# Batch 0's middle feature by the FFT, folds kept out of steps with DFT sums, loads behind the gate, gathers on SyncE's queue

## The chip, the cores and the metric

The kernel runs on one core of a Trainium2 chip. A core has five engines with instruction queues of their own: TensorE (PE: matmuls, with weight loads shown apart as PEld), VectorE (DVE), ScalarE (ACT), GpSimd (POOL) and SyncE (SP, which here only issues DMA transfers). ScalarE and GpSimd issue transfers as well. An engine works through its queue in order, so an instruction that waits holds all that stand behind it. The metric is the device time of one execution in microseconds, lower is better.

## The reference, cut to what matters

```python
x: (8, 3136, 256) float32            # B, S, D
X = np.fft.fft(np.fft.fft(x, axis=1), axis=2).real       # over the sequence, then over the features
h = np.maximum(X @ w_in, 0.0)                             # w_in: (256, 1024)
conv = conv_w[0] * h[s-1] + conv_w[1] * h[s] + conv_w[2] * h[s+1]   # per channel, zero beyond the ends
out = (h * (1 / (1 + np.exp(-conv)))) @ w_out             # w_out: (1024, 256)
```

The three weights arrive as float64, and the kernel narrows them itself.

## The kernel before, in words

**The transform.** The real part of the two-dimensional transform is a cosine-cosine sum minus a sine-sine sum. The kernel uses the symmetries of both. For one batch, rows n of x are folded with their mirror rows (S/2-n and so on) and feature d with feature D-d; what is left are 8 groups of 98 or 99 rows by 128 features, in two tiles `w` per batch. These `fold_ops` (line 143) are 14 pieces per batch, seven for each half h of the rows, nearly all of it VectorE (lines 158 to 187). Then 8 units of four matmuls each (`units`, line 272) multiply the folded rows with cosine and sine tables `tab` over the sequence ("DFT sums"; they accumulate in the single PSUM bank `pd`, for batch 0 in banks `po`); each unit ends with a copy on ScalarE (`u.copy`, lines 287, 306) and two VectorE instructions (`u.fin`, lines 291 to 324) that write a quarter of the rows `pt` (cosine part) and `qt` (sine part), 128 features by 1569 frequencies. The transform over the features is merged into w_in: `G` is the feature table `dm` times w_in (`blocks`, line 589).

**Feature D/2 = 128** has no partner in the fold. Its cosine transform over the sequence is one row of 1569 numbers per batch, and its share of the result is that row times one column `ge` per channel (`column`, line 606). There are two ways to the row in the kernel before:
- Batches 1 to 7: `Feature` (line 374). The 3136 values of one batch are gathered from HBM as a 56 by 56 matrix (`gather`, line 417: 3136 pieces of 4 bytes, issued from ScalarE's queue). Four stages follow: matmul, multiply by twiddles on VectorE, four matmuls, copy and store on ScalarE (lines 443 to 463). `place` (line 380) and `tables` (line 423) prepare its small tables in steps 5 and 11 to 13. Batches 1 to 3 are gathered in step 7, 4 to 7 in step 20.
- Batch 0: the fold keeps x[:, 128] apart (`ea`), `feature` (line 327) multiplies it by the cosine table in 8 small matmuls, GpSimd joins the parts in `er`, `flip` and `store` finish the row.

From the DRAM row `ed`, `spread` (line 465) broadcasts a chunk to all 128 partitions, `eb`. In every step ScalarE then writes eb times ge into the PSUM bank `pa` (`seed`, line 635), and the matmuls add to it. The first four steps of batch 0 have no seed: a fourth matmul with `er` and `left` stands in (lines 661, 662), since the row is not there yet.

**The steps.** The rest is a loop over 256 steps, written out by hand (lines 861 to 885): 8 batches, 4 chunks of the mirrored frequencies (CUTS, line 34), 8 channel tiles. A batch is 32 steps (`per`). For step t the engines get, in this order of the program:
- ScalarE: sigmoid of step t-2 (line 713), copies of the products of step t+1 (line 677, for the first 20 steps lines 672 and 674), the seed of step t+2 (line 643), the first tap of the convolution of step t (line 694).
- VectorE: two additions that make h for k and S-k (line 688), work on the side ("dve"), two further taps of step t-1 (line 700), half of the gating product of step t-2 (line 721).
- GpSimd: the other half of the gating product (line 720).
- TensorE: the products of step t+1 into `pb` and `pa`, six (in the last chunk of odd batches seven) matmuls with w_out of step t-3 into `po`, and at the end the side work "pe": DFT sums of the next batch.

The side work is placed by the dictionary `side`: `at(step, where, fn)`. Where "load" stands, transfers are issued: plain loads and broadcasts from SyncE's queue, and four indirect loads of mirrored rows per half batch from GpSimd (line 133). In the kernel before, "load" stands ahead of "dve" and so ahead of the gate on GpSimd's queue. Folds of batch b run from the end of those of b-1 up to step `stop` (20, 44, 68, 98, 130, 162, 194), its DFT sums from there to step 32b-3 (lines 810 to 841), so that folds of one batch and sums of another share steps.

**The head.** Ahead of the loop: x of batch 0 and the tables are loaded, and a memset on GpSimd (line 577) holds the tables behind the loads of x on SyncE's queue; 16 matmuls keep TensorE busy (`keep_on`, line 750); the folds, the DFT sums of batch 0 and the narrowing of the weights (`narrow`, lines 517 to 524, seven VectorE instructions for 512 columns) follow.

Of the kernel before, what the change touches and what calls it, by code (L numbers as in the profile page):

```python
# [9 lines left out]
F32 = mybir.dt.float32  # L10
# [20 lines left out]
FIRST = 4  # L31
# [7 lines left out]
def kernel(  # L39
# [33 lines left out]
    ep = ctx.enter_context(tc.tile_pool(name="ep", bufs=2))  # L73
    erp = ctx.enter_context(tc.tile_pool(name="erp", bufs=1))
# [28 lines left out]
    xh, wt, ea = {}, {}, {}  # L103
# [3 lines left out]
    sg = const.tile([P, 2, 2], F32, name="sg")  # L107
    nc.gpsimd.memset(sg[:, 0], -1.0)
    nc.gpsimd.memset(sg[:, 1], 1.0)
# [33 lines left out]
    def fold_ops(b):  # L143
# [3 lines left out]

        def half(h):
# [27 lines left out]
            def feats(odd):  # L176
                def f():
                    if h == 0 and odd:
                        wt[b] = [wp.tile([P, 4, HQ, P], F32, name="w", tag="w%d" % i) for i in range(2)]
                        if b == 0:  # L180
                            ea[b] = ep.tile([P, 2, HQ], F32, name="ea", tag="ea")
                            nc.gpsimd.memset(wt[b][0][0:KR, 2:4, :, P - 1:P], 0.0)
# [6 lines left out]
                    if b:  # L189
                        nc.gpsimd.memset(wt[b][odd][k, 2:4, qs, P - 1:P], 0.0)  # L190
                    elif odd:
                        gt(w[k, 2:4, qs, P - 1], t()[k, 7:5:-1, :, P], sg[k], op=ALU.mult)
                    else:
                        nc.gpsimd.tensor_copy(ea[b][k, :, qs], v[:, :, :, P])
# [10 lines left out]
    PQ, eb, er = {}, {}, {}  # L205
# [36 lines left out]
    class Unit:  # L242

        def __init__(self, b, mms, copy, fin, own=False):
            self.own, self.b, self.mms, self.copy_, self.fin_ = own, b, mms, copy, fin

        def matmuls(self, i, n):
            if i == 0:
                self.p = spare() if self.b == 0 and not self.own else psd.tile([P, 512], F32, name="pd", tag="pd")
# [22 lines left out]
    def units(b):  # L272
# [54 lines left out]
        def feature():  # L327

            mms = []
            for i in range(2):  # L330
                for j, qs in enumerate(((3, 1), (2, 0))):
                    for c in range(2):
                        n = HO // 2 + 1 - c
                        o = 32 * (2 * j + c)
                        mms.append(product((slice(o, o + 1), slice(0, n)),
                                           lambda k, q, c=c: ea[b][0:k, c, q:q + 1], 0, qs[i],
                                           slice(c, HE, 2), i == 0, i == 1))

# [613 lines left out]
```

## Time and profile before

| what | value | where from |
|---|---|---|
| median of 3 runs | 1238.14 us (1236.81 to 1238.31) | the times |
| the profiled execution | 1238.29 us, of it span 1236.5 us | the times and the page |
| TensorE busy | 1189.9 us, 96% | page, part 1 |
| VectorE busy | 1136.0 us, 92% | page, part 1 |
| ScalarE busy | 878.1 us, 71% | page, part 1 |
| GpSimd busy | 378.4 us, 31% | page, part 1 |
| chain that ended last | TensorE 71%, VectorE 18%, issue 4%, ScalarE 3% | page, part 4 |
| granted TensorE clock | 0.996 over the span | the times |

All times inside the profile count from the start of the span; 1.8 us of the execution lie outside it. "Busy" for TensorE is not TensorE at its peak, because matmuls overlap and their ends are modelled. The 32nd, 64th, ... gating product of VectorE (line 721) ends at 236.9, 384.8, 530.4, 674.9, 819.5, 964.0 and 1104.1 us; these marks cut the trace into stretches of 32 steps. The first gating product ends at 65.6 us.

### The profile page before, as it was taken

How to read it: one execution, taken by the hardware profiler on the slowest of the kernel's cores; microseconds unless marked ns; L12 is line 12 of the kernel's file. 1: busy time of each engine (PE TensorE's matmuls, PEld its weight loads, DVE VectorE, ACT ScalarE, POOL GpSimd, SP SyncE). 2: the span in 40 equal slices, each digit the busy share in tenths (PEclk: the TensorE clock that was granted, in tenths of full speed). 3: DMA queues.
4: the chain of work that ended last, by engine and by line, in shares of the span. 5: the costliest groups of instructions: out<-in, count | busy, mean ns of one | idle time of the engine just before them, and what ended most of it. 6: DMA issues, size and time to landing. Idle time of an engine off the chain costs nothing.

```text
span 1236.5 us, 15434 instructions
## 1 busy us (share of the span) xinstructions
PE 1189.9 (96%) x4876; PEld 908.4 (73%) x4876; DVE 1136.0 (92%) x1696; ACT 878.1 (71%) x1832; POOL 378.4 (31%) x474
## 2 busy tenths in 40 slices
PE   5998989899999999999999999999999999999998
PEld 4666667677777777677777777777777777777776
DVE  7799979999999989999999999999899888899996
ACT  2467646686677776777777777787777777788884
POOL 5225431433324241342324223242122211222222
PEclk9999999999999999999999999999999999999999
DMA  9504241211222120210212111120001000110000
GB/s 226 183 7 79 79 55 46 85 28 52 65 66 76 33 65 14 75 56 26 79 38 67 31 52 52 45 86 26 9 18 52 31 26 27 39 39 27 26 27 30
DMA packets 70213, 66.30 MB, mean 54 GB/s; under 512 B 28123, under 2 KB 57827, under 8 KB 70131
## 3 DMA queue, kind: packets, MB, share of 16 engines
q1 hardware_dynamic: 42443, 52.09, 13.7%
q0 software_dynamic: 5120, 12.85, 3.5%
q10 hardware_dynamic: 22568, 0.36, 1.3%
q8 instruction: 39, 0.64, 0.2%
q14 instruction: 43, 0.35, 0.1%
HBM read 39.53 MB, written 25.74 MB: 53 GB/s over the span
## 4 chain that ended last, share of the span: by engine, by line
PE 71%; DVE 18%; issue 4%; ACT 3%; DMA 1%; ACTq 0%; SPq 0%; DVEq 0%
PE po L94 43%; PE pb L94 10%; PE pa L94 10%; PE pd L94 7%; DVE g L700 6%; DVE g L721 2%; DVE h L688 2%; DVE xh L158 2%; ACT nb L677 1%; DVE w L187 1%; DVE xh L169 1%; DVE w L186 1%; DMA xh<-in_x_dram 1%; ACT g L713 1%; ACTq L419 0%
## 5 line engine op out<-in xcount | busy, mean ns | idle before, releaser
L94 PE MATMUL po<-wout,g 128*128 128x256 f32 x3072 | 711.6, 381 | 18.2 <-DVE g L721 18.2
L94 PEld LDWEIGHTS po<-wout,g 128*128 128x128 f32 x3072 | 580.8, 190 | 173.0 <-DVE g L721 50.0
L700 DVE SCALAR_TENSOR_TENSOR g<-h,cw,g 128x770 f32<-128x770 f32 (+1 forms) x512 | 555.5, 1085 | 9.8 <-ACT g L694 0.7
L720 POOL TENSOR_TENSOR g<-g,h 128x385 f32<-128x385 f32 (+1 forms) x256 | 241.0, 942 | 793.3 <-ACT g L713 536.3
L713 ACT ACTIVATE g<-g 128x385 f32<-128x385 f32 (+2 forms) x512 | 244.4, 527 | 200.7 <-DVE g L700 199.5
L677 ACT ACTIVATE nb<-pb 128x386 f32<-128x386 f32 (+2 forms) x472 | 208.2, 494 | 81.4 <-PE pb L94 80.5
L688 DVE CUSTOM_DVE_ANT_0 h<-pa,nb 128x386 f32<-128x386 f32 (+2 forms) x492 | 255.5, 559 | 3.7 <-ACT h L674 3.7
L694 ACT ACTIVATE g<-h,cw 128x770 f32<-128x770 f32 (+1 forms) x256 | 243.6, 951 | 0.2 <-DVE h L688 0.2
L94 PE MATMUL pa<-pt,G 128*128 128x387 f32 (+2 forms) x512 | 212.5, 496 | 7.5 <-ACT pa L643 7.5
L94 PE MATMUL pb<-qt,G 127*128 127x387 f32 (+2 forms) x512 | 212.6, 496 | 0.0
L643 ACT ACTIVATE pa<-eb,ge 128x387 f32<-128x387 f32 (+2 forms) x252 | 151.8, 603 | 15.8 <-issue 11.6
L94 PEld LDWEIGHTS pa<-pt,G 128*128 128x128 f32 x512 | 96.6, 189 | 82.1 <-issue 18.6
L721 DVE TENSOR_TENSOR g<-g,h 128x385 f32<-128x385 f32 (+1 forms) x256 | 145.4, 568 | 1.4 <-ACT g L713 1.4
L94 PE MATMUL pd<-tab,w 98*128 98x196 f32 (+3 forms) x448 | 120.9, 374 | 0.0
L94 PEld LDWEIGHTS pb<-qt,G 127*128 127x128 f32 x512 | 94.7, 190 | 17.4 <-issue 1.0
L133 POOL DMA_INDIRECT xh<-in_x_dram,idx x64 | 97.9, 1529 | 15.4 <-issue 13.0
L94 PEld LDWEIGHTS pd<-tab,w 98*128 98x128 f32 (+1 forms) x448 | 83.6, 190 | 12.7
L740 ACT COPY os<-po 128x256 f32<-128x256 f32 x196 | 58.2, 394 | 8.5 <-PE po L94 5.5
L158 DVE TENSOR_TENSOR xh<-xh 98x1020 f32<-98x1020 f32 (+1 forms) x32 | 46.7, 1465 | 3.8 <-DMA xh<-in_x_dram,idx 3.8
L169 DVE TENSOR_TENSOR xh<-xh 98x1024 f32<-98x1024 f32 (+1 forms) x32 | 40.6, 1269 | 0.1
L188 POOL COPY w<-xh 98x4 f32<-98x4 f32 (+1 forms) x32 | 27.4, 856 | 13.3 <-DVE xh L174 7.4
L291 DVE TENSOR_TENSOR qt<-as,pd 128x197 f32<-128x197 f32 (+1 forms) x14 | 7.2, 514 | 19.9 <-ACT as L287 19.9
(114 smaller groups left out, 392.8 us busy)
## 6 DMA issues: line engine op xcount, KB each, us to landing
out_dram<-os SPq DMA_DIRECT2D x192, 128.0 KB
xh<-in_x_dram SPq DMA_DIRECT2D x16, 784.0 KB
eb<-ed SPq DMA_DIRECT2D x16, 193.5 KB
tab<-dft_seq_dram SPq DMA_DIRECT2D x4, 589.5 KB
raw<-in_moe_w_in_dram SPq DMA_DIRECT2D x4, 512.0 KB
raw<-in_moe_w_out_dram SPq DMA_DIRECT2D x1, 2048.0 KB
eb<-ed SPq DMA_DIRECT2D x8, 209.0 KB
eb<-ed SPq DMA_DIRECT2D x8, 193.0 KB
```

Of the source, the lines that this page charges most:

```text
L94: nc.tensor.matmul(o, l, r, start=start, stop=stop, skip_group_check=True)
L133: nc.gpsimd.indirect_dma_start(out=xh[b, h][0:NP, 7 - m].rearrange("p q d -> p (q d)"), out_offset=None, in_=bass.AP(tensor=x.tensor, offs ...
L158: vt(a[:, :, :, 1:D], a[:, :, :, 1:D], r[:, :, :, D - 1:0:-1], op=ALU.add)
L643: act(pa[s][:, 0:n], eb[b, c], AF.Copy, scale=ge[:, f:f + 1])
L677: act(nb[s][:, i, cols], p[:, cols], AF.Copy, scale=-1.0 if i else 1.0)
L688: nc.vector._custom_dve(TENSOR_ADD_SAT, out=to, in0=a[:, cols], in1=c[:, i, cols], s0=BIG, s1=0.0)
L694: act(gs[s], hs[s][:, 0:n], AF.Copy, scale=cw[:, 0, s[2]:s[2] + 1])
L700: stt(out=g, in0=h[:, k:k + n], scalar=cw[:, k, f:f + 1], in1=g, op0=ALU.mult, op1=ALU.add)
L713: act(gs[s][:, c], gs[s][:, c], AF.Sigmoid)
L720: gt(g[:, p], g[:, p], h[:, p], op=ALU.mult)
L721: vt(g[:, v], g[:, v], h[:, v], op=ALU.mult)
L740: nc.scalar.copy(out=osb[:, j % 2], in_=pt[:, j % 2])
```

## The change

- Batch 0's row for feature D/2 comes from `Feature` too. `place` and `tables` move into the head, as does one gather; stages 0 and 1 are put between the folds (after 11 of 14 pieces), stage 2 behind `keep_on`, stage 3 behind the first `mirror_tables`. `feature`, `row`, `flip`, `store`, `ea`, `er` and the fourth matmul of the first four steps go, and these steps get seeds like all others. `keep_on` is 8 matmuls of 512 columns in place of 16 of 256, two of them into the two `pa` banks; the matmuls that had started those banks (`start_all`) go.
- On SyncE's queue the broadcast of batch 0's first chunk is put ahead of the loads of `dm` and of w_in's parts 1 to 3, which had stood directly behind the tables. The columns of `ge` for the first channel tiles are computed ahead of the loop.
- All gathers are issued from SyncE's queue, one per step (steps 6 to 8 and 21 to 24).
- "load" is run behind the gate instead of ahead of "dve", and the loads of a half batch are spread over one step each.
- The ends of the folds are 20, 46, 72, 98, 125, 157, 189. A fold piece of batch 2 or later takes the next step that holds no `u.fin`, no stage 1 of `Feature` and no other fold piece (`free`). The steps of the folds become: batch 2: 20, 28, 30, 31, 33 to 40, 42, 44; batch 3: 46, 48, 50, 52, 54, 56, 58, 60, 62, 63, 64, 66, 68, 70; batch 4: 72, 73, 75, 78, 80, 81, 83, 86, 88, 89, 91, 92, 94, 96; and so on. Batch 1's stay in steps 9 to 19.

```diff
-FIRST = 4
-                        if b == 0:
-                            ea[b] = ep.tile([P, 2, HQ], F32, name="ea", tag="ea")
-                            nc.gpsimd.memset(wt[b][0][0:KR, 2:4, :, P - 1:P], 0.0)
...
-                    if b:
-                        nc.gpsimd.memset(wt[b][odd][k, 2:4, qs, P - 1:P], 0.0)
-                    elif odd:
-                        gt(w[k, 2:4, qs, P - 1], t()[k, 7:5:-1, :, P], sg[k], op=ALU.mult)
-                    else:
-                        nc.gpsimd.tensor_copy(ea[b][k, :, qs], v[:, :, :, P])
+                    nc.gpsimd.memset(w[k, 2:4, qs, P - 1:P], 0.0)
...
-        def gather(self, b0, b1):
-            for b in range(b0, b1):
-                nc.scalar.dma_start(out=self.y[self.K, b - b0].unsqueeze(2), in_=bass.AP(
-                    tensor=x.tensor, offset=x.offset + b * S * D + P,
-                    ap=[[RC * D, RC], [D, RC], [1, 1]]))
+        def gather(self, b, b0):
+            nc.sync.dma_start(out=self.y[self.K, b - b0].unsqueeze(2), in_=bass.AP(
+                tensor=x.tensor, offset=x.offset + b * S * D + P, ap=[[RC * D, RC], [D, RC], [1, 1]]))
...
+    feat = Feature()
     w_cv.load(nc.scalar)
+    feat.place()
     for h in range(2):
         for f in load_ops(0, h, nc.sync, nc.scalar, h == 1):
             f()
+    feat.gather(0, 0)
 
     nc.gpsimd.memset(tabs[1][0:1, 0, 0, 0:1], 0.0)
     load_tables(1)
     w_in[0].load(nc.sync)
     load_tables(0)
-    nc.sync.dma_start(out=dm, in_=dft_dim[:, :, 0:2])
-    for i in (1, 2, 3):
-        w_in[i].load(nc.sync)
...
-        if not first(s):
-            if s in ((0, 0, FIRST), (0, 0, FIRST + 1)):
-                start_all(pa[s].rearrange("p (t n) -> p t n", t=2), dm[:, 0, 0], w4[0])
-            act(pa[s][:, 0:n], eb[b, c], AF.Copy, scale=ge[:, f:f + 1])
+        act(pa[s][:, 0:n], eb[b, c], AF.Copy, scale=ge[:, f:f + 1])
...
-        if first(s):
-            mm(pa[s][:, 0:n], left[0:1, f, :], er[b][:, ch.k0:ch.k1], False, False)
...
-    for f in fold_ops(0):
+    for i in range(3):
+        feat.tables(i)
+    begin, us = units(0)
+    begin()
+    ops = fold_ops(0)
+    for f in ops[0:11]:
         f()
+    feat.stage(0, 0, 1)
+    feat.stage(1, 0, 1)
+    for f in ops[11:]:
+        f()
 
-    odds = [us[j] for j in (0, 1, 5, 6)]
+    odds = [us[j] for j in (0, 1, 4, 5)]
     w_in[0].narrow(0, 2)
-    keep_on(16)
+    keep_on([idle] * 6)
+
+    keep_on([psa.tile([P, 512], F32, name="pa", tag="pa") for _ in range(2)])
+    feat.stage(2, 0, 1)
     mirror_tables(0)
+    feat.stage(3, 0, 1)
+    spread(0, [0])
+    nc.sync.dma_start(out=dm, in_=dft_dim[:, :, 0:2])
+    for i in (1, 2, 3):
+        w_in[i].load(nc.sync)
...
-    flip()
-    store()
-    spread(0, range(len(chunks)))
+    spread(0, range(1, len(chunks)))
     for f in load_ops(1, 0, nc.sync):
         f()
+    column(0)
     blocks(0)
...
+    ends = [9] + [max(26 * b - 6, per * (b - 1) - 3) for b in range(1, B)]
+    taken = set()
+
+    def free(cycle):
+
+        while cycle in taken:
+            cycle += 1
+        taken.add(cycle)
+        return cycle
+
+    for c, b0, b1 in ((6, 1, min(4, B)), (21, 4, B)):
+        for b in range(b0, b1):
+            at(c + b - b0, "load", lambda b=b, b0=b0: feat.gather(b, b0))
+    for c, b0, b1 in ((14, 1, min(4, B)), (per - 1, 4, B)):
+        for i, where in enumerate(("pe", "dve", "pe", "act")):
+            at(c + i + (i > 2), where, lambda i=i, b0=b0, b1=b1: feat.stage(i, b0, b1))
+        taken.add(c + 1)
...
+        c0, n = ends[b - 1], ends[b] - ends[b - 1]
+        cs = [free(c0 + j * n // len(ops)) if b > 1 else c0 + j * n // len(ops) for j in range(len(ops))]
...
+                for j, fn in enumerate(load_ops(b + 1, h, nc.sync)):
+                    at(cs[7 * h + 6] + 1 + j, "load", fn)
...
         if t < n:
             combine(steps[t])
-        run("load")
         run("dve")
...
         if 0 <= t - 2 < n:
             gate(steps[t - 2])
+        run("load")
         if t >= LAG:
             mm2(steps[t - LAG])
         run("pe")
```

## The prediction

> **What bounds the kernel now.** I read the page first, for the two engines that are nearly full, then the busy time in stretches of 32 steps (their marks are in the section above), then the places where TensorE stands idle, in order of time. From the page:
>
> ```profile
> PE 1189.9 (96%) x4876; PEld 908.4 (73%) x4876; DVE 1136.0 (92%) x1696; ACT 878.1 (71%) x1832; POOL 378.4 (31%) x474
> ...
> PE 71%; DVE 18%; issue 4%; ACT 3%; DMA 1%; ACTq 0%; SPq 0%; DVEq 0%
> ```
>
> TensorE bounds most of the span, but not all: 18% of the chain is VectorE. Where, the stretches tell (start:end, length, busy time of PE, PEld, DVE, ACT, POOL, then granted clock, DMA share, GB/s):
>
> ```profile
> 65.60:236.90 171.30, 157.87 (x633) 115.75 (x631) 158.06 (x224) 108.02 (x236) 62.48 (x73) 0.99 0.28 59
> 236.90:384.80 147.90, 145.99 (x595) 112.06 (x596) 140.70 (x214) 108.12 (x224) 47.61 (x60) 0.99 0.16 50
> 384.80:530.40 145.60, 141.90 (x580) 108.15 (x579) 137.60 (x210) 107.40 (x224) 49.55 (x59) 1.00 0.19 58
> ...
> 819.50:964.00 144.50, 142.60 (x588) 109.98 (x588) 135.20 (x208) 107.73 (x224) 37.96 (x50) 1.00 0.10 32
> 964.00:1104.10 140.10, 140.10 (x582) 109.11 (x581) 120.36 (x185) 107.44 (x224) 29.08 (x40) 1.00 0.10 30
> ```
>
> The stretch from 964.00 has DFT sums but no folds, and TensorE never stops: 140.1 us is what TensorE needs for an even batch. An odd one has 8 more output matmuls of 0.43 us, 3.5 us, so 143.6. Against these floors the stretches from 236.9 on (147.9, 145.6, then 144.5, 144.6, 144.5) stand 4.3, 5.5, 0.9, 4.5 and 0.9 us too high: 16.1 us is all that better placed folds can bring there. The first stretch has VectorE and TensorE equally full and 13.4 us of idle TensorE. Its largest piece, from the timeline (start, us, engine, line):
>
> ```profile
> 157.16 2.90 ACTq L419 DMA_DIRECT2D ft<-in_x_dram  x1
> ...
> 160.10 4.58 ACTq L419 DMA_DIRECT2D ft<-in_x_dram  x2
> ...
> 164.74 0.59 ACT L643 ACTIVATE pa<-eb,ge 128x387 f32<-128x387 f32 x1 [6.78 <-issue]
> ...
> 165.38 1.36 PE L94 MATMUL pa<-pt,G 128*128 128x387 f32 x2 [3.78 <-ACT pa L643]
> ...
> 166.53 4.04 PE L94 MATMUL po<-wout,g 128*128 128x256 f32 x12
> ```
>
> ScalarE issues four gathers, stands 6.78 us behind them, and the seed (L643) comes late; TensorE waits 3.78 us for it. Then its clock is down: the stretch 165 to 170 shows a granted 0.66, and twelve records that take 2.75 us elsewhere take 4.04, the two before them 1.36 instead of 0.81. The stall costs 3.78 + 1.29 + 0.55 = 5.6 us.
>
> What a fold does in a step with sums, VectorE's timeline in step 54:
>
> ```profile
> 326.93 1.02 DVE L688 CUSTOM_DVE_ANT_0 h<-pa,nb 128x386 f32<-128x386 f32 x2
> 328.97 0.36 DVE L310 TENSOR_TENSOR as<-as,pd 128x196 f32<-128x196 f32 x1 [1.02 <-ACT as L306]
> 329.25 0.35 DVE L312 TENSOR_TENSOR as<-as,pd 128x196 f32<-128x196 f32 x1
> 329.52 0.68 DVE L186 TENSOR_TENSOR w<-xh 98x508 f32<-98x508 f32 x1
> 330.12 0.68 DVE L187 TENSOR_TENSOR w<-xh 98x508 f32<-98x508 f32 x1
> 330.71 2.07 DVE L700 SCALAR_TENSOR_TENSOR g<-h,cw,g 128x770 f32<-128x770 f32 x2
> 332.70 0.56 DVE L721 TENSOR_TENSOR g<-g,h 128x385 f32<-128x385 f32 x1
> ```
>
> The end of the sums waits for ScalarE's copy (1.02 us), which waits for TensorE; so VectorE is tied to TensorE there, and the fold of 1.3 us lies on the way to the taps and the gate. The step takes 6.24 us from gate to gate, its neighbours without side work 3.43. The next steps with a fold alone take about 4.7, which TensorE's step (six output matmuls 2.59, two products 1.30, some 0.5 of sums) nearly covers.
>
> **The head, part by part.** Its chain: the tables land, ScalarE mirrors (L239), TensorE sums, VectorE narrows and finishes.
>
> ```profile
> 26.05 8.10 PE L94 MATMUL po<-tab,w 98*128 98x196 f32 x32
> ...
> 36.65 0.88 PE L94 MATMUL pd<-tab,ea 99*1 99x197 f32 x16
> ...
> 46.04 0.91 PE L94 MATMUL pa<-er,left 1*128 1x386 f32 x2
> ...
> 58.17 0.56 DVE L688 CUSTOM_DVE_ANT_0 h<-pa,nb 128x385 f32<-128x385 f32 x1 [2.82 <-ACT h L674]
> ```
>
> *Added.* `place` on GpSimd took 1.93 us in step 5 (76.61 to 78.54) and now stands ahead of the eight indirect loads of x; the memset that releases the tables follows these, so the tables are issued at 14.8 instead of 12.90. One gather goes ahead of them: four gathers filled the DMA engines from 155 to 170 us (shares 0.97, 0.95 and 0.46 of 5 us, 11.9 us), less about 3.4 us for the 0.8 MB of x in the first of these stretches: 2.1 us each. The small tables (0.18 MB at the head's 240 GB/s) are 0.8 us. The engines were idle for parts of the first 12 us, so these overlap: the tables come between 1.5 and 4 us later, I take 2.7. TensorE's sums then start at 28.7 instead of 26.05. Stages 0 to 3 themselves are short (matmuls of 0.3 us, products 0.5 x 2 on VectorE, ACT copy 0.3) and lie in waits for the tables; four more seeds on ScalarE (0.59 each) lie in its idle time, as it is busy 6.5 of the 15 us from 40 to 55. If that cover is gone they cost 2.4.
>
> *Moved on SyncE's queue.* The broadcast of chunk 0 waits for the store of stage 3: `mirror_tables` ends at 25.9 + 2.7 = 28.6, copy and issue 0.6, and 1.6 to land (the row's store of before was issued at 43.39, the broadcast behind it at 44.96): 31. Behind it stand `dm`, three parts of w_in and w_out. Part 1 (0.26 + 0.52 MB at 240 GB/s, 3.3 us, and 1.6 to land) is there at 36; VectorE narrows it at 36.28 + 2.7 = 39. It is covered by 3 us.
>
> *Removed.* On TensorE 0.88 (`ea`), four products of 0.65, two blocks of about 0.43 and two starts of 1.02, some 6 us, most of it between 44 and 64 us, where VectorE waits: 2.82 us at 58.17 and 0.84 at 48.42. VectorE's chain from 26 to 58 us is otherwise full, so it moves by +2.7 and loses 3.66 in waits; I keep 0.25 of that as lost to the new order and book **-0.7 us** (between +1 and -3).
>
> **The loop.** *Gathers.* The second group saves **-5.6 us** (-3.5 if the sums behind it, where TensorE is the bound, take part of it back; -7.3 if VectorE's own idle time counts). The first group (5.29 us of ScalarE at 89.72) meets a stretch where VectorE is full with narrowing; VectorE waited 0.50 there (at 96.53), and 0.17 of `place` (L402) leaves its way: **-0.7** (0 to -3, as TensorE lost 2.83). The seven transfers now hold SyncE, whose next work, stores and broadcasts, is steps away. Here the Trainium skill speaks against the edit: "DMA: Bandwidth & Descriptors", section "Issuing engines are not separate DMA queues", says that all queues share the same 16 engines and that another issuer saves only the sequencer's issue time, usually small. By the rule these two items are worth about 0 and the sum below would be 1229. The row decides: the issue held ScalarE for 5.29 and 8.3 us, presumably at the pace at which the pieces were moved, and SyncE can stand that.
>
> *Loads behind the gate.* GpSimd's loads (median 1.50 us) no longer delay its gate product (0.87). No instruction of TensorE waits longest for L720 before, so nothing is gained: 0. What is late now is the load itself, by one step of 4.5; the fold that uses the tile is seven pieces away.
>
> *Folds.* Collisions of fold and sums: about five per batch go, at about 0.9 us each (the excess of 4.5 in an even stretch over five). But folds are packed: VectorE per stretch is 24 x 3.43 + 8 x 3.72 = 112.1 plus 1.31 per piece (9.15 us for seven) plus 7.4 for sums. Stretch by stretch:
> - 236.9: 20 pieces, VectorE 146.5 with the two stage-1 products: it, not TensorE, is the bound. It was 147.9 with 19 pieces, of which a step with a fold and stage 1 at 231 to 237 cost a clock drop (0.74). I take 146.4: **-1.5** (+3 to -4.3).
> - 384.8: 17 pieces, VectorE 141.8 and waits: 143.6, **-2.0** (0 to -5.5).
> - 530.4: floor 143.6 plus a little, **-0.7**; 819.5 the same, **-0.7**.
> - 674.9: 14 pieces, VectorE 137.8, so TensorE's 140.1 plus 0.9: **-3.6** (-1 to -4.5).
> - From 964 no folds, before and after: 0. In steps 20 to 29 TensorE is the bound with its dense sums, so four pieces fewer there bring nothing.
>
> **Sum.** -0.7 - 5.6 - 0.7 - 1.5 - 2.0 - 0.7 - 3.6 - 0.7 = -15.5 us. The profiled execution took 1238.29, 1236.5 in the span; that it stands 0.15 above the median of the runs is nothing. 1238.3 - 15.5 = **1222.8 us**.
>
> **Rivals.**
> 1. *VectorE becomes the bound.* Ten folds in the eleven steps from 30 to 40 need 4.74 us a step where TensorE needs 3.9, 8 us in all; waits at the end of the sums add 1 us each time. Then the stretches from 236.9 give nothing together, and the gathers and the head remain: -7.0, **1231**. For it: DVE 140.70 of 147.90. Against it: VectorE may lag by more than a step before TensorE starves.
> 2. *Everything reaches its floor.* All of the 16.1, the whole 7.3 and 1 to 3 more in the head: **1213**. Against it: 17 and 20 pieces in a stretch.
> 3. *SyncE's queue stalls the head, slower.* Place: the broadcast that waits for the stored row, with part 1 of w_in behind it. Price: one us of the head for each us after the 3 us of cover. With 15.5 us of gain elsewhere it decides when the row lands later than about 49 us instead of 31; 23 us of delay give **1243**. Nothing in the trace has a small store land so late.
> 4. *No change.* The stall is given back: TensorE is full with sums in steps 20 to 29 whoever issues, and the head loses 4 us: **1238**. Against it: the 3.78 us of idle TensorE and the clock.
>
> **How the numbers follow.** This kernel's measurement can tell about 0.2%, 2.5 us. Chances: forecast 0.62 (own range 1217 to 1229), rival 1 0.2, rival 2 0.1, rival 3 0.04, rival 4 0.04. The range 1213 to 1233 leaves out some of rivals 2, 3 and 4 and the far end of 1. Faster 0.93, within 0.03, slower 0.04.
>
> **What would show it.** After: no idle of ScalarE for issue longer than 1 us; no step with a PE clock of 0.66; the five middle stretches at 146, 144, 144, 141 and 144; TensorE's sums in the head at 28 to 29; VectorE's wait of 2.82 gone. It is wrong if sums start later than 31, if w_in's part 1 holds VectorE, or if TensorE's waits for L721 grow in steps 30 to 45.

## The result and the profile after

| | before | after |
|---|---|---|
| median of the runs | 1238.22 us (1236.81 to 1238.47) | 1227.74 us (1226.35 to 1228.34) |
| ratio to before, 95% interval | | 0.9916 [0.9899, 0.9933] |
| the profiled execution, and its span | 1238.29, 1236.5 us | 1227.89, 1226.1 us |

The kernel is 10.5 us faster; 15.5 had been forecast. From the page of the kernel after, busy times and shares of the chain that ended last:

```profile
PE 1180.9 (96%) x4834; PEld 900.0 (73%) x4834; DVE 1126.7 (92%) x1698; ACT 876.0 (71%) x1830; POOL 362.1 (30%) x466
...
PE 71%; DVE 21%; issue 4%; ACT 2%; DMA 1%; POOL 0%; DVEq 0%; SPq 0%; POOLq 0%; ACTq 0%
```

TensorE still does most of the chain; VectorE's share has gone up from 18% to 21%, although it has less to do. Where the time went is read from the stretches of 32 steps, cut at the same gating products as before (columns: start:end, length, busy time of PE, PEld, DVE, ACT, POOL, granted clock, DMA share, GB/s):

```profile
69.30:231.10 161.80, 152.77 (x620) 112.20 (x620) 150.21 (x216) 103.09 (x213) 52.41 (x60) 1.00 0.21 51
231.10:379.80 148.70, 145.25 (x592) 110.38 (x592) 141.25 (x217) 107.58 (x225) 54.30 (x64) 1.00 0.19 60
379.80:525.30 145.50, 142.48 (x581) 108.25 (x580) 138.47 (x212) 107.40 (x225) 44.09 (x58) 1.00 0.18 57
525.30:670.50 145.20, 144.94 (x599) 111.66 (x599) 137.56 (x212) 107.42 (x225) 53.21 (x60) 1.00 0.17 56
670.50:813.20 142.70, 141.49 (x582) 108.63 (x581) 134.65 (x207) 108.08 (x224) 45.78 (x56) 1.00 0.16 52
813.20:956.00 142.80, 142.52 (x590) 110.51 (x589) 131.42 (x205) 108.00 (x224) 30.31 (x48) 1.00 0.08 29
956.00:1093.80 137.80, 137.80 (x570) 107.10 (x569) 121.03 (x183) 106.73 (x224) 30.78 (x40) 1.00 0.09 30
```

Set against the stretches before, and against the forecast:

| part | before | forecast | after | after less before |
|---|---|---|---|---|
| up to the first gating product | 65.6 | 64.9 | 69.3 | +3.7 |
| first stretch | 171.3 | 165.0 | 161.8 | -9.5 |
| second | 147.9 | 146.4 | 148.7 | +0.8 |
| third | 145.6 | 143.6 | 145.5 | -0.1 |
| fourth | 144.5 | 143.8 | 145.2 | +0.7 |
| fifth | 144.6 | 141.0 | 142.7 | -1.9 |
| sixth | 144.5 | 143.8 | 142.8 | -1.7 |
| seventh | 140.1 | 140.1 | 137.8 | -2.3 |
| last | 132.4 | 132.4 | 132.3 | -0.1 |

The parts add up to the spans, 1236.5 and 1226.1 us, and differ by 10.4. So three things need an answer: a head that lost 3.7 us instead of winning 0.7, a first stretch that won 3.2 more than booked, and stretches two to seven, where the folds act, that won 4.5 us instead of 8.5.

The gathers did what was said. SyncE's timeline of the kernel after, where the last three gathers of the second group are issued (start, us, engine, line):

```profile
162.92 5.27 SPq L361 DMA_DIRECT2D ft<-in_x_dram  x3
```

TensorE's timeline of the kernel after, same place:

```profile
162.64 0.82 PE L91 MATMUL pa<-pt,G 128*128 128x387 f32 x2
163.29 2.75 PE L91 MATMUL po<-wout,g 128*128 128x256 f32 x12
165.88 2.80 PE L91 MATMUL pd<-tab,w 98*128 98x392 f32 x8
```

They hold SyncE for 5.27 us, and nothing on TensorE waits: there is no bracket with an idle time in these rows, and twelve output matmuls take 2.75 us again instead of 4.04.

The head did not. The chain that ended last, followed through the head of the kernel after (start, us, what):

```profile
8.87 12.15 DMA ft<-in_x_dram
21.15 0.59 PE pd L91 x2
21.74 8.53 PE pb L91 x12
30.28 1.72 PE pa L91 x4
31.99 0.51 PE pd L91 x8
32.50 8.13 PE po L91 x32
```

The gather of batch 0 is issued at 8.87 and is 12.15 us away. Stage 0 (`pd`, the second row) waits for it, and on TensorE's queue the warm-up (`keep_on`, twelve records into `pb` and four into `pa`, 10.25 us) stands behind stage 0. The sums of batch 0 (`po`) follow at 32.5. Before, the warm-up waited for a folded tile `w` only, and the sums followed it at 26.05; from TensorE's timeline of the kernel before:

```profile
15.84 10.38 PE L94 MATMUL pb<-w 98*128 98x256 f32 x32 [9.41 <-POOL w L188]
```

The late sums hold VectorE, which stands 6.10 us before it can finish the first of them (1.86 us at this place before). From its timeline of the kernel after:

```profile
39.38 0.36 DVE L295 TENSOR_TENSOR as<-as,po 128x196 f32<-128x196 f32 x1 [6.10 <-ACT as L291]
```

### The profile page after: what moved, and what is told of

Its sections match the earlier page's. It is cut to its first block, busy times and chain, and to the rows that moved or that the text cites. A ratio compares the mean times of both kernels' runs of the same rounds, so it can differ in the third digit from the quotient of the medians.

```text
span 1226.1 us, 15361 instructions
## 1 busy us (share of the span) xinstructions
PE 1180.9 (96%) x4834; PEld 900.0 (73%) x4834; DVE 1126.7 (92%) x1698; ACT 876.0 (71%) x1830; POOL 362.1 (30%) x466
## 4 chain that ended last, share of the span: by engine, by line
PE 71%; DVE 21%; issue 4%; ACT 2%; DMA 1%; POOL 0%; DVEq 0%; SPq 0%; POOLq 0%; ACTq 0%
PE po L91 43%; PE pb L91 11%; PE pa L91 10%; PE pd L91 7%; DVE g L623 7%; DVE h L611 3%; DVE g L644 3%; DVE xh L151 2%; DVE xh L162 1%; DMA ft<-in_x_dram 1%; ACT nb L600 1%; DVE w L176 1%; DVE w L177 1%; DVE xh L166 0%; DVE pt L276 0%
## 5 line engine op out<-in xcount | busy, mean ns | idle before, releaser
L623 DVE SCALAR_TENSOR_TENSOR g<-h,cw,g 128x770 f32<-128x770 f32 (+1 forms) x512 | 548.9, 1072 | 9.3 <-ACT g L617 0.2
L643 POOL TENSOR_TENSOR g<-g,h 128x385 f32<-128x385 f32 (+1 forms) x256 | 231.4, 904 | 794.9 <-ACT g L636 535.6
L636 ACT ACTIVATE g<-g 128x385 f32<-128x385 f32 (+2 forms) x512 | 244.4, 527 | 206.7 <-DVE g L623 206.1
L568 ACT ACTIVATE pa<-eb,ge 128x387 f32<-128x387 f32 (+2 forms) x256 | 154.0, 602 | 0.7 <-ACT ft L402 0.6
L127 POOL DMA_INDIRECT xh<-in_x_dram,idx x64 | 106.2, 1659 | 14.4 <-issue 11.1
L151 DVE TENSOR_TENSOR xh<-xh 98x1020 f32<-98x1020 f32 (+1 forms) x32 | 41.3, 1292 | 4.5 <-DMA xh<-in_x_dram 2.9
L178 POOL COPY w<-xh 98x4 f32<-98x4 f32 (+1 forms) x32 | 18.2, 570 | 25.3 <-DVE xh L162 11.8
```

The lines of the kernel that those rows point to most:

```text
L127: nc.gpsimd.indirect_dma_start(out=xh[b, h][0:NP, 7 - m].rearrange("p q d -> p (q d)"), out_offset=None, in_=bass.AP(tensor=x.tensor, offs ...
L151: vt(a[:, :, :, 1:D], a[:, :, :, 1:D], r[:, :, :, D - 1:0:-1], op=ALU.add)
L568: act(pa[s][:, 0:n], eb[b, c], AF.Copy, scale=ge[:, f:f + 1])
L623: stt(out=g, in0=h[:, k:k + n], scalar=cw[:, k, f:f + 1], in1=g, op0=ALU.mult, op1=ALU.add)
L636: act(gs[s][:, c], gs[s][:, c], AF.Sigmoid)
L643: gt(g[:, p], g[:, p], h[:, p], op=ALU.mult)
```

## The experiments

The theory at the start was the prediction's own sum with one correction from the traces: the head is not late because the tables are late alone, but because work waits in two queues, TensorE's (the warm-up behind stage 0) and SyncE's (dm and w_in behind the broadcast that waits for the stored row; rival 3's mechanism). Its rivals: the folds, not the head, are what fell short; or the head is short of something that no order changes.

### The head

**The old head with the changed loop.** The kernel before with the changed gathers, loads, ends and folds of the loop; batch 0 keeps `feature`, `row` and its first four steps without seeds.

> The kernel before with the changes of the loop alone (folds in free steps, loads behind the gate, gathers from SyncE's queue), and with its own head and its own way to batch 0's feature. Theory A (the loop gains 14, the head of the changed kernel loses 3.7): 1224.0, first gating product at 65.6. Rival (the new head's seeds and the small tables loaded early relieve the first 32 steps, so the loop gains less without them): 1227.7 or more, with the first stretch of 32 steps at 165 or more instead of 161.8.

Measured 1223.06 us (1222.26 to 1223.65), ratio 0.9871 [0.9855, 0.9888]: faster than the whole change by 4.7 us between the medians, the intervals of the ratios apart. Its first gating product ends at 65.0 us, and all its stretches equal those of the changed kernel within 0.3 us, the first with 161.8 too: theory A holds, the rival does not. By the medians the loop's part of the change is worth some 15.5 us, and the new head loses 4.7 of them.

**Warm-up ahead of stage 0.**

```diff
+    keep_on([idle] * 6)
     feat.stage(0, 0, 1)
     feat.stage(1, 0, 1)
...
     w_in[0].narrow(0, 2)
-    keep_on([idle] * 6)
```

> The changed kernel with six of the eight warm-up matmuls put ahead of stage 0 on TensorE's queue, so that they no longer stand behind the gather of batch 0. Theory A (stage 0, waiting for the gather until 21.1 us, holds the warm-up, which ends at 31.9 and so delays the sums): the sums start at 29.1 to 29.6 instead of 32.4, the first gating product ends 3 us earlier (66.3 instead of 69.3), time 1224.7. Theory B (the tables, which land 3.2 us later than before, set the head, the warm-up only fills the wait): sums start unchanged at 32.4, time 1227.7.

Measured 1228.97 us (1227.48 to 1229.72), ratio 0.9917 [0.9900, 0.9933]: no gain. The sums did start early, at 26.42 instead of 32.43. But the first gating product came at 71.1 us, for VectorE now stood elsewhere. Its timeline:

```profile
41.88 0.43 DVE L458 TENSOR_SCALAR win<-raw 128x512 int32<-128x512 int32 x1 [4.86 <-DMA raw<-in_moe_w_in_dram]
...
55.97 0.56 DVE L611 CUSTOM_DVE_ANT_0 h<-pa,nb 128x385 f32<-128x385 f32 x1 [3.40 <-ACT h L597]
```

It waits 4.86 us for part 1 of w_in, which SyncE had issued behind the broadcast (at 35.61). One wait had hidden the other: theory A was right on why the sums were late, and wrong on what that was worth.

**Loads ahead of the broadcast, warm-up as changed.**

```diff
-    spread(0, [0])
     nc.sync.dma_start(out=dm, in_=dft_dim[:, :, 0:2])
     for i in (1, 2, 3):
         w_in[i].load(nc.sync)
+    spread(0, [0])
```

> The changed kernel with dm and the rest of w_in issued ahead of the broadcast, and nothing else: the warm-up stays behind the first stage. Theory A (limits in series, the sums' start at 32.4 binds here and the loads are not late): first gate 68.5 to 69.3, time 1226.9 to 1227.7. Rival C (the loads behind the stored row are the whole loss, as a stalled queue): first gate near 65, time near 1223.3.

Measured 1225.42 us (1225.20 to 1226.06), ratio 0.9894 [0.9879, 0.9909], first gating product at 67.4. That is 1.9 us better than the changed kernel in the profile, between the two expectations. But 1.5 of it are there before a load can matter: the gather happened to land at 19.7 instead of 21.1, so the sums started at 30.92 instead of 32.43. The intervals of the two ratios overlap, and the first product of five kernels with the changed kernel's head as it is (the changed one and four below: 69.3, 68.3, 69.7, 69.4, 71.4) spreads by 3 us. Theory A expected no gain at all and rival C 4.4 us; a gain of the loads alone is not shown.

**Both.** Warm-up ahead of the stages and loads ahead of the broadcast.

> As the run with the warm-up ahead of the stages, and dm and the rest of w_in are issued on SyncE's queue ahead of the broadcast of the stored row. Theory A (two limits in series: the warm-up behind the first stage on TensorE, and SyncE's queue behind the stored row; lifting one only uncovers the other): VectorE's wait for w_in part 1 (4.86 us with the warm-up alone moved) is gone, the first step's gate comes near 65 us as with the old head (65.0) instead of 69.3, and the time is near 1223.3 (1227.7 less 4.4). Rival B (the loads put earlier take the DMA engines from the tables, or a third limit such as the broadcast itself holds the first step): the gate stays at 68 to 70 and the time at 1226.5 to 1228.5.

Measured 1226.39 us (1222.75 to 1226.99), ratio 0.9894 [0.9876, 0.9913]; first product at 67.6. Against the warm-up alone this is 3.5 us at the first product and 2.6 us in the median, though the intervals of the two ratios overlap; the trace shows the cause at work, as VectorE's wait for part 1 has gone from 4.86 to 2.72 us. But 65.0 is not reached, and against the loads alone (67.4, the same ratio, with a gather that happened to land early) the early warm-up has brought nothing that can be seen: theory A got only part of the way, and rival B's third limit is there. VectorE's timeline of this kernel:

```profile
39.81 0.43 DVE L458 TENSOR_SCALAR win<-raw 128x512 int32<-128x512 int32 x1 [2.72 <-DMA raw<-in_moe_w_in_dram]
```

SyncE's:

```profile
14.62 2.48 SPq L204 DMA_DIRECT2D tab<-dft_seq_dram  x2
...
25.62 0.64 SPq L210 DMA_DIRECT2D tab<-dft_seq_dram  x1
26.31 0.62 SPq L698 DMA_DIRECT2D dm<-dft_dim_dram  x1
26.97 4.38 SPq L480 DMA_DIRECT2D raw<-in_moe_w_in_dram  x3
```

The same transfers with the old head and the changed loop:

```profile
13.47 1.40 SPq L219 DMA_DIRECT2D tab<-dft_seq_dram  x2
...
19.59 0.63 SPq L225 DMA_DIRECT2D tab<-dft_seq_dram  x1
21.91 0.62 SPq L579 DMA_DIRECT2D dm<-dft_dim_dram  x1
22.58 2.92 SPq L537 DMA_DIRECT2D raw<-in_moe_w_in_dram  x3
```

The table transfers start 1.15 us later, but the last of them is issued 6.03 us later, after a wait for earlier ones to land, and w_in 4.4 us later. VectorE runs late from its wait for part 1 on. So the tables themselves land late. Either the 3136 elements stand ahead of them on SyncE's queue, or the DMA engines are full.

**Which of the two?** Two more orders of batch 0's gather, both with the two edits above: ahead of x on SyncE's queue, and ahead of x on ScalarE's (shown is what comes on top of the two edits; for SyncE it is without the last argument).

```diff
+    feat.gather(0, 0, nc.scalar)
     for h in range(2):
         for f in load_ops(0, h, nc.sync, nc.scalar, h == 1):
             f()
-    feat.gather(0, 0)
```

> As the run with both limits lifted, and batch 0's gather of 3136 elements issued on SyncE's queue ahead of x instead of behind it. Theory E (the elements move only from 13 to 19 us because x is ahead of them on the queue; sent first they land by about 10 and stage 0 waits for tables alone, while x comes 2 us later and its folds have slack behind TensorE's tables): first gate 0 to 1.5 us earlier than with both limits lifted, time 1222 to 1223.3. Rival F (x and the folds are what the sums wait for, and every element sent ahead of x delays them): first gate 1 to 4 us later, 1224 to 1227.

> As the run with both limits lifted (warm-up ahead of the stages, loads ahead of the broadcast), and batch 0's gather issued on ScalarE's queue ahead of x. Theory G (the 3136 elements stand ahead of the tables on SyncE's own queue, so that the second table's last transfer is held until 25.6 us and w_in part 1 lands 2.7 us late; on another queue they hold nothing): that transfer is issued by 22, VectorE's wait for w_in part 1 is under 0.5 us, first gate 64.5 to 65.5, time 1223.2 to 1224.5. Rival H (the elements take the DMA engines from x and the tables on whatever queue): VectorE still waits 2 to 3 us for part 1, first gate 67 to 68.5, time 1225.5 to 1227.

Ahead of x on SyncE: 1227.48 us (1224.98 to 1228.50), ratio 0.9909 [0.9892, 0.9926], first product at 68.2. On ScalarE's queue: 1225.74 us (1223.93 to 1228.03), ratio 0.9887 [0.9872, 0.9903], first product at 68.9, the last table transfer still at 26.52 and VectorE's wait for part 1 still 2.40 us. Theory G is wrong: the queue is not it. Rival H's wait of 2 to 3 us came; the gather ahead of x (theory E) did not bring the first product earlier than 67.6. What the elements cost shows where they run undisturbed, busy times of the kernel that gathers on ScalarE's queue (the last two columns are the DMA share and GB/s):

```profile
8.00:12.00 4.00, 0.00 (x0) 0.00 (x0) 1.22 (x1) 1.26 (x1) 3.17 (x5) 1.00 1.24 125
```

The kernel before in the same and the following stretches:

```profile
8.00:12.00 4.00, 0.00 (x0) 0.00 (x0) 2.44 (x3) 0.00 (x0) 3.08 (x4) 1.00 0.92 253
12.00:16.00 4.00, 0.16 (x1) 0.16 (x1) 3.90 (x6) 0.00 (x0) 3.83 (x6) 1.00 1.05 220
16.00:20.00 4.00, 4.00 (x10) 3.19 (x11) 3.96 (x6) 0.00 (x0) 1.30 (x2) 1.00 1.00 247
```

And the changed kernel:

```profile
12.00:16.00 4.00, 0.00 (x0) 0.00 (x0) 3.93 (x6) 0.53 (x5) 2.32 (x5) 1.00 1.12 203
16.00:20.00 4.00, 0.00 (x0) 0.00 (x0) 3.93 (x6) 0.00 (x0) 0.75 (x2) 1.00 0.99 172
```

From 12 to 28 us the DMA engines are full in all three kernels. Where the elements pass, full engines move 125 or 172 GB/s instead of 220 to 253: with the gather's issue just ahead of this stretch, 4 us times (253 - 125) are 512 KB not moved, by estimate 2.1 us at 245 GB/s. The small tables of `Feature` add two transfers of 86 KB, 0.7 us. Together that is an estimate of 2.8 us more of DMA work ahead of w_in's part 1; VectorE waits 2.09 to 2.72 us for it in the three kernels with both edits. Summed from such rows, the DMA engines had moved 4.4 MB by 20 us with the old head (the kernel before, and its head with the changed loop) and 3.8 to 3.9 MB with the new one, wherever the gather stood. That none of the three orders helps is shown; that the bytes and elements are the cause is the reading of these rows. A head with `Feature` and without its gather was not tried, nor one without its other new work: TensorE's columns of `ge` ahead of the first products (1.02 us at 47.60) and the seeds of the first four steps, of which one (0.58 us at 56.87) stands on the chain that ended last.

### The gathers and the loads behind the gate

Three kernels, all with the changed head, ends and folds. In the first, batches 1 to 7 are gathered from ScalarE's queue as before (three in step 7, four in step 20), with "load" behind the gate as changed. In the second, "load" stands ahead of "dve" again as well. In the third only "load" is put back, and the gathers stay on SyncE's queue.

```diff
-    for c, b0, b1 in ((6, 1, min(4, B)), (21, 4, B)):
+    for c, b0, b1 in ((7, 1, min(4, B)), (20, 4, B)):
...
-            at(c + b - b0, "load", lambda b=b, b0=b0: feat.gather(b, b0))
+            at(c, "load", lambda b=b, b0=b0: feat.gather(b, b0, nc.scalar))
...
+        run("load")
         run("dve")
...
             gate(steps[t - 2])
-        run("load")
```

> The changed kernel with the loop's gathers issued from ScalarE's queue again, three in step 7 and four in step 20, as before; batch 0's stays on SyncE's. Theory of the prediction (the issue holds ScalarE, the seed is late, TensorE waits and its clock drops): +6.3 us, 1234.0, and a wait of ScalarE for issue of some 6 us in the profile. Rival (the rule that the issuing queue saves little, since all share the same engines): 1227.7 to 1228.7.

> Gathers of batches 1 to 7 on ScalarE's queue as before (three in step 7, four in step 20), and side loads issued ahead of the fold and the seed as before: of the gathers' part, the change is undone whole; ends, folds and head stay as changed. Theory A (the gathers' price on ScalarE depends on what stands behind them: ahead of the seed it is the 6.3 us of the prediction, behind the seed 3.1): time 1234.0 (1227.7 plus 6.3), first stretch 168.1. Rival D (the price is 3.1 wherever they stand): 1230.8, first stretch 165.0.

> The changed kernel with its side loads put back ahead of the fold and the seed, and nothing else; all gathers stay on SyncE's queue. Theory A (the loads' place matters only to DMAs that ScalarE issues; on SyncE's queue it is worth nothing): first stretch 161.8, time 1227.2 to 1228.3. Rival I (loads behind the gate gain or lose in themselves, as transfers of x then start up to 5 us later): 1225.5 or 1230.

| gathers | "load" | us | ratio | first stretch |
|---|---|---|---|---|
| SyncE, one a step | behind the gate (changed kernel) | 1227.74 | 0.9916 [0.9899, 0.9933] | 161.8 |
| SyncE, one a step | ahead of "dve" | 1229.26 | 0.9914 [0.9898, 0.9929] | 162.0 |
| ScalarE, together | behind the gate | 1230.78 | 0.9941 [0.9924, 0.9958] | 165.0 |
| ScalarE, together | ahead of "dve" | 1233.71 | 0.9959 [0.9945, 0.9972] | 168.4 |

The times of the first and third rows have overlapping intervals; the first stretch separates them, as it is 161.8 us in all six kernels that have the new head and the changed gathers, "load" and folds. The queue alone missed both of its expectations (1234.0, and 1227.7 to 1228.7); with both edits undone, theory A of the second run holds. The two edits are not independent. ScalarE's timeline with "load" ahead of "dve":

```profile
162.63 4.51 ACTq L361 DMA_DIRECT2D ft<-in_x_dram  x2
167.19 0.59 ACT L568 ACTIVATE pa<-eb,ge 128x387 f32<-128x387 f32 x1 [6.71 <-issue]
```

And with "load" behind the gate:

```profile
158.10 0.59 ACT L568 ACTIVATE pa<-eb,ge 128x387 f32<-128x387 f32 x1
...
158.88 6.38 ACTq L361 DMA_DIRECT2D ft<-in_x_dram  x3
165.30 0.94 ACT L636 ACTIVATE g<-g 128x385 f32<-128x385 f32 x2 [5.76 <-issue]
```

In both ScalarE stands some 6 us. In the first case the seed (L568) stands behind the gathers and TensorE waits 3.71 us for it; in the second the seed and the first tap have gone ahead, only the sigmoid (L636) and what follows it are late, and TensorE waits 2.94 us. TensorE's timeline in the first case:

```profile
167.82 1.66 PE L91 MATMUL pa<-pt,G 128*128 128x387 f32 x2 [3.71 <-ACT pa L568]
169.27 3.47 PE L91 MATMUL po<-wout,g 128*128 128x256 f32 x12
```

And in the second:

```profile
168.02 2.87 PE L91 MATMUL pd<-tab,w 98*128 98x392 f32 x8 [2.94 <-DVE as L297]
...
172.04 2.75 PE L91 MATMUL po<-wout,g 128*128 128x256 f32 x12
```

The clock makes part of the difference. In the first case the granted clock is 0.73 from 168 to 173 us, and fourteen records take 1.57 us longer than elsewhere (0.81 and 2.75 us); in the second it stays at 1.00 from 165 to 175. The stretch is 6.6 us longer than the changed kernel's in the first case and 3.2 in the second. So the two edits together bring 6.6 us (6.0 by the medians), against 6.3 in the forecast. What one of them brings depends on the other: "load" 3.4 us while ScalarE gathers and 0.2 once SyncE does, the queue 6.4 us while "load" is early and 3.2 once it is late. The 0.2 is theory A of the third run; the 1.5 us between its median and the changed kernel's are no more than its head was late in the profile (first product at 71.4 instead of 69.3).

The rest of the first stretch's 9.5 us, 2.9 us, comes back in none of these kernels, nor with the old folds (161.9, below). The last section has a likely place for it.

### The folds

**The old ends and steps of the folds**, with everything else as changed.

```diff
-    ends = [9] + [max(26 * b - 6, per * (b - 1) - 3) for b in range(1, B)]
+    ends = [9] + [per * (b - 1) + max(28 - 8 * b, 2) for b in range(1, B)]
...
-        cs = [free(c0 + j * n // len(ops)) if b > 1 else c0 + j * n // len(ops) for j in range(len(ops))]
+        cs = [c0 + j * n // len(ops) for j in range(len(ops))]
```

> The changed kernel with the folds and DFT sums in the steps of before, folds again in steps with sums; head, gathers and loads as changed. The prediction's terms for the folds (1.5 + 2.0 + 0.7 + 3.6 + 0.7): +8.5, 1236.2. The two traces, stretch by stretch behind step 32: +4.4, 1232.1. Rival (folds in separate steps gain nothing, what the stretches show comes from elsewhere): 1227.7 within 1.

Measured 1231.34 us (1230.24 to 1233.01), ratio 0.9939 [0.9923, 0.9956]: the new folds bring 3.6 us by the medians, not 8.5; the intervals of the two ratios overlap a little, so the stretches decide. Its stretches two to seven are 146.9, 145.9, 144.0, 145.5, 144.0 and 140.2 against 148.7, 145.5, 145.2, 142.7, 142.8 and 137.8: with the old folds the second is 1.8 us shorter, the third 0.4 longer, and the last four are 5.2 us longer together, 3.8 in all.

**The folds of batches 2 and 3 at their old steps, those of 4 to 7 at free steps.** Once with the old head, once with the head that has both edits and the gather on ScalarE's queue.

```diff
-    ends = [9] + [max(26 * b - 6, per * (b - 1) - 3) for b in range(1, B)]
+    ends = [9] + [per * (b - 1) + 28 - 8 * b if b < 4 else max(26 * b - 6, per * (b - 1) - 3) for b in range(1, B)]
...
-        cs = [free(c0 + j * n // len(ops)) if b > 1 else c0 + j * n // len(ops) for j in range(len(ops))]
+        cs = [free(c0 + j * n // len(ops)) if b > 3 else c0 + j * n // len(ops) for j in range(len(ops))]
```

> The old head with the changed loop, and the folds and sums of batches 2 and 3 at their old steps, those of batches 4 to 7 at the changed ones. Theory A (the four folds that the change moves from steps 20 to 28 to steps 30 to 40 cost 1.8 us there, where TensorE has no sums and VectorE sets the pace; the later batches' moves gain 5.1): the stretch of steps 33 to 64 falls from 148.7 to 146.9, the next rises by 0.4, time 1221.7 (1223.1 less 1.4). Rival J (the two parts do not add, since batch 4's folds then follow at other steps): 1223 to 1225.

> As the run with both limits lifted and the head's gather on ScalarE's queue, with the folds and sums of batches 2 and 3 at their old steps. If both gains hold: 1.4 us under that run, 1221.8 to 1223. If the head stays at a first gate of 67.5: 1224.5 to 1225.5.

With the old head 1219.39 us (1218.84 to 1219.92), ratio 0.9839 [0.9825, 0.9852]. This is the fastest kernel of the study: 20.1 us under the kernel before in the same runs, and by the ratios (0.9839 against 0.9916, their intervals apart) some 9.5 us under the changed one. With the new head 1222.80 us (1220.22 to 1223.97), ratio 0.9859 [0.9844, 0.9874], first product at 69.0. The first gained more than expected, 3.7 us by the medians against the old head with the changed folds, where 1.4 had been forecast; the second lies in its expected range. The stretches of the first of the two:

```profile
64.40:226.20 161.80, 156.19 (x638) 115.12 (x637) 154.70 (x224) 108.27 (x237) 59.34 (x71) 1.00 0.28 60
226.20:373.10 146.90, 144.29 (x591) 110.47 (x591) 138.83 (x213) 107.78 (x224) 50.31 (x62) 1.00 0.17 53
373.10:517.00 143.90, 141.98 (x580) 108.22 (x579) 136.31 (x210) 107.30 (x225) 44.79 (x56) 1.00 0.19 57
```

The first stretch holds six more VectorE instructions than with the same head and the changed folds (218), and is no longer; the second holds four fewer and is 1.8 us shorter; the third two fewer and 1.6 us shorter, which had been expected 0.4 longer and is not explained. What the packed folds cost is seen in the eight steps after the mark. The changed kernel:

```profile
231.10:267.30 36.20, 33.42 (x131) 24.24 (x131) 35.92 (x53) 26.35 (x57) 16.87 (x21) 1.00 0.21 68
```

The kernel with the mixed folds:

```profile
226.20:259.50 33.30, 32.47 (x131) 24.30 (x131) 32.45 (x48) 26.33 (x57) 12.77 (x19) 1.00 0.12 38
```

TensorE has the same 131 records in both. In the changed kernel VectorE is busy for 35.92 of 36.20 us with five more instructions, and TensorE waits six times for its gating product, 2.8 us in all, against twice and 0.8 us in the other. Of these 2.9 us the next steps give back 1.1.

## Why the prediction was right or wrong

- **Sign and size.** 10.5 us against 15.5, inside the range and inside the forecast's own range. The shortfall of 5 us is the sum of a head 4.4 worse, folds 4.0 worse and a first stretch 3.2 better. That the total came so near is in part luck: for the loop alone 14.8 had been booked and 14.0 came in the stretches, because the first stretch won nearly what the folds missed. By the time alone, 1227.7, the sum without the gathers (1229) would have been nearer than 1222.8; only the runs tell that the gathers did what was said.
- **The head (-0.7, measured +3.7) is the step that failed.** Its first half held: the tables came later, as ScalarE's `mirror_tables` began at 27.13 instead of 23.95, 3.2 us later where 2.7 had been taken. Then "TensorE's sums then start at 28.7" was wrong; they started at 32.43, beyond the 31 that the text had set as its own refutation. Stage 0 had been costed by its duration (0.3 us a matmul, "lie in waits for the tables"), not by its place: it waits on TensorE's queue for the gather until 21.15, and the 10 us of warm-up stand behind it. Second, part 1 of w_in, "there at 36" and "covered by 3 us", took the loads as landing at 240 GB/s from a quiet queue. With the warm-up put ahead, part 1 came only at 41.88, 4.86 us late, when it stood behind the stored row, and still 2.1 to 2.7 late when it did not. Third, the estimate of 2.1 us of DMA time for one gather agrees with the rows, but it was booked once, for the tables; w_in stands behind them, and even with both edits it was issued 4.4 us later than with the old head. Lifting the first two did not bring the loss back: the first product went from 69.3 to 67.6, with 65.0 for the old head. What holds the rest is the late landing of tables and w_in; that the gather's bytes cause it is likely, and stays open. The four seeds, booked at nothing under cover, are on the chain once with 0.58 us.
- **Rival 3** had the place (SyncE's queue behind the stored row) and the rule of its price, a microsecond for each one beyond the 3 us of cover. It asked for 23 us of delay because it was weighed against the whole gain; 4.86 us of it came as soon as the warm-up was early. It cost nothing in the changed kernel, only because the sums were later still.
- **The gathers (-5.6 and -0.7) were right**, in cause and size: 6.6 us when the gathers and the order of "load" are both undone, with the late seed, TensorE's wait and the lower clock of the forecast. The share of the first group was not measured apart. The rule of the Trainium skill that had been weighed ("DMA: Bandwidth & Descriptors", section "Issuing engines are not separate DMA queues": another issuer saves only the sequencer's time, usually small beside the transfer itself) would have made this 0. It is true of the transfers, as the head shows, where moving one gather to another queue brought nothing; but here the sequencer's time is 5 to 8 us (5.27 us on SyncE for three gathers, 8.3 on ScalarE before), and what stood behind it was on TensorE's path.
- **Loads behind the gate (0)** were right for the changed kernel (0.2 us), for a reason not given. The forecast looked at GpSimd's product alone; while ScalarE issues the gathers, the place of "load" decides whether the seed stands behind them, and is worth 3.4 us. The other edit had taken that away.
- **The folds (-8.5) were mis-sized**: -4.5 in the stretches, -3.6 by the run that undoes them. For the second and third stretch, -3.5 was booked and +0.7 measured. "In steps 20 to 29 TensorE is the bound with its dense sums, so four pieces fewer there bring nothing" held; that they would cost nothing in steps 30 to 40 did not. Rival 1 was right in its place and too high in its price: about 1.8 us net, not 8. The seventh stretch was called TensorE's floor of 140.1 us and became 137.8: it has 570 matmul records instead of 582, because batch 7's sums now start before its mark. The bound of a stretch is no floor when work can cross its mark.
- **What was to be seen after**: in the loop no issue of a transfer keeps ScalarE waiting (idle times of 3.48 and 1.82 us put down to issue stand in the head only), and the clock of 0.66 is gone, as said; VectorE's wait of 2.82 is gone too, though one of 6.10 has come earlier. The sums at 28 to 29 us were not seen, and of the middle stretches at 146, 144, 144, 141, 144 none within a microsecond (148.7, 145.5, 145.2, 142.7, 142.8). Of the three signs of being wrong two came: the late sums, and TensorE's waits for the gating product in steps 30 to 45, which grew from 3.0 us in two waits to 3.9 in eight.

## What to carry to other kernels

Cost an instruction that is put into another engine's order by what it waits for and by what stands behind it in its queue, not by its duration: here 0.6 us of matmuls put off the first sums by 6 us. When one wait is lifted, look at once for the wait that it had covered; here lifting the first left the time where it was. An issue that takes microseconds belongs on the queue behind which nothing urgent stands. In a stage where the DMA engines are full, the rows suggest that a gather of single elements is paid for in lost bytes by the transfers behind it, on whatever queue it is issued; a stage where the engines are idle is the place to try for it. Side work is best placed where the engine that does it is not the bound: four folds among dense sums cost nothing, the same four in steps without sums cost 1.8 us.

## What the runs showed that was not expected

- **VectorE's instructions lengthen while GpSimd's gating product runs.** VectorE's timeline of the kernel before:

```profile
78.09 1.56 DVE L519 TENSOR_SCALAR wout<-wout 128x512 int32<-128x512 int32 x1
...
130.58 2.45 DVE L158 TENSOR_TENSOR xh<-xh 99x1020 f32<-99x1020 f32 x1
```

GpSimd's at the same times:

```profile
77.36 1.18 POOL L411 MEMSET ft<- 1x393 f32 x4
...
78.50 0.85 POOL L720 TENSOR_TENSOR g<-g,h 128x385 f32<-128x385 f32 x1
...
131.06 0.88 POOL L720 TENSOR_TENSOR g<-g,h 128x385 f32<-128x385 f32 x1
```

The first takes 0.43 us elsewhere (L460 of the changed kernel), 1.13 less; the second 1.20 us, 1.25 less. Each overlaps a gating product (L720) and ends a little less than its usual time after the product has ended (at 79.35 and 131.94 us), as if it had been held until then. It is the product that counts: of the 32 executions of L158, the ten that overlap no product take 1.21 to 1.22 us, four of them with an indirect load of GpSimd beside them, and those that overlap one take up to 2.45. In the changed kernel these two collisions are gone, and others have come (at 139.81 us a fold of 0.68 takes 1.55 beside the product at 139.96). Summed over the first stretch, each instruction against the median of its own form without a product beside it, the lengthening is 12.4 us before, 9.8 in the changed kernel and 9.6 in the kernel with gathers and "load" both undone, whose first stretch lacks 2.9 us against before. So 2.8 us of this lengthening went with those 2.9 us; that it is their cause is likely, and no run isolates it. The move of `place` into the head is not needed for it: with the old head, which keeps `place` in the loop, the first stretch is 161.8 as well. The Trainium skill ("SBUF — State Buffer", section "SBUF: two separate sides") says that VectorE and GpSimd share one pair of ports under an exclusive lock: of an operation of VectorE with two inputs from SBUF and one of GpSimd that reads SBUF, the one that starts first blocks the other for its whole length. The fold and the product are such a pair, and a fold held to the product's end agrees with it; but by the records the fold at 130.58 starts 0.48 us ahead of the product, and it is the fold that is longer, while the product takes 0.88 us, no more than its mean of 0.94. For an instruction with one input, as L519, the page names a 2-port mode of VectorE as the condition, which no run here shows.
- **A gather of 3136 single elements lands late**: 12.15 us from its issue when x stands ahead of it, though SyncE needs 1 us to issue it; later ones in one batch took SyncE 15.87 us for three (from 43.77 in the changed kernel), at no harm, as nothing near waited for SyncE.
- **The new head varies**: five kernels with the same head had their first gating product between 68.3 and 71.4 us, while their stretches two to seven agreed within 0.3 us wherever the folds were the same.
